# Idle products, SBUF-loaded tap diagonals and two moved loads at the start, two moved sums at the end, of a gated S5/H3 mix

## The chip, the cores and the metric

The kernel runs on one core of a Trainium2 chip. The metric is the time of one execution in device microseconds (us); lower is better. The core has five engines that run their own instruction streams: TensorE (PE; its weight loads are shown apart as PEld), VectorE (DVE), ScalarE (ACT), GpSimd (POOL) and SyncE (SP). DMAs are issued from the instruction streams of SP, ACT and POOL.

## The reference, cut to what matters

```python
x = A_x                                            # [1, 2048, 1024], bfloat16
g = sigmoid((x * gate_w).sum(-1, keepdims=True))
# a: a diagonal complex state space model with 1024 states
dt = exp(log_dt); Lam = Lambda_re + 1j * Lambda_im
Lam_bar = exp(dt * Lam); B_bar = ((Lam_bar - 1) / Lam)[:, None] * (B_re + 1j * B_im)
h[t] = Lam_bar * h[t - 1] + B_bar @ x[t]           # 2048 steps
a = 2 * real(h @ Cmat.T) + x * Dskip
# b: four taps along time, a product, a long convolution over 2048 steps, a product
k_shift[t] = sum(k[t - i] * shift_k[:, i] for i in range(4))
kv = k_shift * v
b = x * (causal_convolution(kv, ssm_k) + kv * ssm_D)
return g * a + (1 - g) * b
```

## The kernel before, in words

Part b works on eight blocks of 128 channels. For a block, `load_k` transposes k into the tile `kk` (channels on partitions, time along the row), and `tap_unit` makes the four taps on TensorE: a diagonal matrix `w` of tap weights times `kk`, shifted by 0 to 3 steps, summed in PSUM (`taps`). For block 0 these are 16 products of 128x128 by 128x512, eight for each half of the time axis; ScalarE copies each half to `ks`. VectorE multiplies `ks` with v (`vT`) in `times_v`. Then the block is folded (`kf`, `vf`, turned by TensorE into `psf` and copied to `eok`, `eov`), taken to its spectrum with tables of cosines and sines (`CF`, `SF`; products `psK`, `psV`, copied to `Kr`, `Ks`, `Vh`), multiplied there on VectorE and taken back (`psz`, `cv`) into a scratch tensor in HBM, `cv_scr`.

Part a cuts the time axis by its remainder r modulo 8, and the states into 16 blocks q of 64, real and imaginary parts on 128 partitions. `B_unit(q)` turns a block of B (`Bst`, loaded by `load_B`) with a small matrix of the columns (`L`, made on VectorE by `matrices`) into `BT`, by way of PSUM `psB` and a copy on ScalarE. `step_unit` multiplies the transposed x (`xT`) with `BT` (`bu`), and the states run through carries, a scan and, last, `Cy`: the states times C into `psy`, one tile of 128 rows of the output after another. `gate(r)` makes the sums for g from `xT` and `gz`.

The start is written out by hand at the end of the function: loads, then `step(ft)` (tables), `vectors()` (a product that turns the rows of log_dt and Lambda into columns, `pcol`), `step(mv)`, `step(sc)` (the state columns `cw`), `step(mv)`, `tap_weights(0)`, the taps of block 0, `gate(0)`, and then B, fold and spectrum of block 0. `more_vectors` (`mv`) turns by 13 small products the rows `skr` (tap weights), gate_w and D (`gsr`) into columns: of `skr` eight for `tcol` (the blocks 1 to 7) and four for `dcol` (block 0), one product for `gz` and `sDc`. `tap_weights(0)` then makes four diagonals on ScalarE from the identity and `dcol`.

Every engine's instructions stand in the order in which the code records them: `put` makes each follow the one before it on its engine. So an instruction that waits holds all that stands behind it on its engine. Nearly every row of the profile therefore has the line of `put`, L99, and the rows are told apart by the names of their tiles. DMAs are issued by `move` (SP), `small` (ACT) and `hop` (POOL). A DMA may also wait for an older one that uses the same counter, of which there are eight for SP and ACT together and eight for POOL.

At the end the last tile of rows is made as two halves of 512 columns, the last two entries of `ends`. For each half `row_scale` (ScalarE) prepares `pair` and `gd` (the scaled convolution and D), and `row_mix` does three things on VectorE: add `gd`, multiply with x, and add the scaled `psy` in a SCALAR_TENSOR_TENSOR; then SP stores the half.

Buffers come from pools by name: `s2` has 33 slots, `psum` four of 128x2x512 in f32.

## Time and profile before

| what | value |
|---|---|
| runs shown | 408.44, 409.61, 413.74 us (median 409.61) |
| the profiled execution | 408.37 us |
| its span, from the first to the last instruction | 406.6 us |
| PE, DVE, ACT, POOL busy | 379.7, 326.7, 251.2, 37.2 us |
| first product on PE, first tap | 5.33 us, 8.81 us |
| last product of PE ends, last store is issued | 401.1 us, 403.51 us |

All times inside a profile count from the span's start. A timeline row has the start, the time from the start to the end of the last of its instructions, the engine (with a q for its instruction queue, which issues DMAs), the line, the operation, the tiles written and read, shapes, how many instructions were merged, and in brackets the engine's idle time before it and what ended that. Matmuls are pipelined, so one lasts longer than the distance to the next.

### The profile page before, as it was taken

To read this page: it belongs to the slowest core of one execution; us is meant where nothing else is said; L and a number is where in the kernel's file an instruction comes from. 1 tells how busy PE (TensorE), PEld (TensorE's weight loads), DVE (VectorE), ACT (ScalarE), POOL (GpSimd) and SP (SyncE) were. 2 spreads that over 40 slices of the span, in tenths; PEclk is the share of its full clock that TensorE was granted. 3 is DMA by queue.
4 is the path that set the end of the run, shared out by engine and by line. 5 is a ranking of instruction groups with operands and counts; after the bars stand their busy time and mean duration, and the time that the engine had idled before them with its cause. 6 is when DMAs were issued, how large, how long until landed. Compare 5 with 4: busy or idle time off the path is not lost.

```text
span 406.6 us, 6769 instructions
## 1 busy us (share of the span) xinstructions
PE 379.7 (93%) x2630; PEld 238.2 (59%) x2630; DVE 326.7 (80%) x421; ACT 251.2 (62%) x321; POOL 37.2 (9%) x77
## 2 busy tenths in 40 slices
PE   2889998999899999999997999978999999999994
PEld 1458976567577768787675775444444444444441
DVE  6853896988969999679694889996897999577554
ACT  5883686856795874695726865385734449265760
POOL 2201000522240221000012000100000000000000
PEclk9999999999999999999999999999999999999999
DMA  8999989999699367905999789995760130888742
GB/s 156 218 209 215 220 179 197 143 223 152 65 222 241 85 122 168 178 21 105 239 205 189 158 147 233 228 151 117 157 188 5 60 84 19 232 264 235 218 122 76
DMA packets 136272, 65.51 MB, mean 161 GB/s; under 512 B 117672, under 2 KB 123824, under 8 KB 136240
## 3 DMA queue, kind: packets, MB, share of 16 engines
q1 hardware_dynamic: 127712, 50.62, 60.5%
q0 software_dynamic: 3888, 6.33, 10.4%
q10 hardware_dynamic: 4640, 8.14, 7.1%
q8 instruction: 20, 0.33, 0.3%
q14 instruction: 12, 0.10, 0.1%
HBM read 19.68 MB, written 11.01 MB: 75 GB/s over the span
## 4 chain that ended last, share of the span: by engine, by line
PE 55%; DVE 8%; ACT 4%; DMA 4%; issue 4%; SPq 1%; ACTq 1%; DVEq 0%; POOLq 0%
PE psy L99 24%; PE bu L99 15%; PE psz L99 4%; PE psV L99 4%; PE psK L99 3%; DVE G L99 3%; PE psT L99 3%; DMA CT<-CT 2%; PE taps L99 2%; ACT h L99 1%; DMA kk<-kk 1%; DVE tmp L99 1%; DVE a L99 1%; SPq L99 1%; DVE T L99 1%
## 5 line engine op out<-in xcount | busy, mean ns | idle before, releaser
L99 PE MATMUL bu<-xT,BT 128*128 128x256 bf16 x1024 | 116.9, 273 | 3.2 <-ACT Kr L99 2.9
L99 PEld LDWEIGHTS <-BT 128*128 128x128 bf16 x1024 | 99.6, 98 | 20.8 <-issue 5.3
L99 PE MATMUL psy<-CT,h 128*128 128x512 bf16 x448 | 98.7, 379 | 2.8 <-DMA CT<-Cim 2.8
L99 PEld LDWEIGHTS <-h 128*128 128x128 bf16 x448 | 43.7, 98 | 56.1 <-DMA CT<-Cim 2.3
L99 ACT ACTIVATE h<-bu 128x1024 bf16<-128x1024 f32 x28 | 28.5, 1022 | 39.1 <-PE bu L99 38.7
L99 ACT ACTIVATE Vh<-psV 128x1024 bf16<-128x1024 f32 x32 | 31.7, 1047 | 4.6 <-PE psV L99 4.6
L99 DVE TENSOR_TENSOR G<-G,tmp 128x3072 bf16<-128x3072 bf16 (+2 forms) x24 | 29.4, 1225 | 0.8
L99 DVE TENSOR_TENSOR T<-T,tmp 128x3072 bf16<-128x3072 bf16 (+2 forms) x24 | 29.4, 1225 | 0.8
L99 ACT ACTIVATE cv<-psz 128x1024 bf16<-128x1024 f32 x16 | 16.4, 1027 | 21.5 <-PE psz L99 10.4
L99 ACT ACTIVATE h<-psT 128x1024 bf16<-128x1024 f32 x28 | 27.9, 1027 | 2.8 <-PE psK L99 1.2
L99 DVE TENSOR_TENSOR tmp<-Kp,Vh 128x3072 bf16<-128x3072 bf16 (+2 forms) x24 | 29.3, 1221 | 0.4
L99 DVE TENSOR_TENSOR G<-Kr,Vh 128x4096 bf16<-128x4096 bf16 x8 | 18.3, 2288 | 12.4 <-ACT Vh L99 12.4
L99 POOL DMA_DIRECT2D kk<-kk x21 | 11.0, 529 | 167.9 <-DMA kk<-in_B_k_dram 110.4
L99 PE MATMUL psT<-h,ident 128*128 128x256 bf16 x112 | 25.6, 273 | 0.0
L99 PEld LDWEIGHTS <-L 128*128 128x128 bf16 x224 | 21.9, 98 | 5.0 <-ACT cv L99 0.7
L99 PE MATMUL psz<-T,CI 128*128 128x512 bf16 x64 | 24.3, 379 | 0.0
L99 PE MATMUL psz<-T,SI 128*128 128x512 bf16 x64 | 24.3, 379 | 0.0
L99 PE MATMUL taps<-kk,w 128*64 128x512 bf16 (+1 forms) x128 | 19.7, 399 | 3.9 <-ACT w L99 2.3
L99 ACT ACTIVATE pairx<-pairx,omg 128x1024 bf16<-128x1024 bf16 (+1 forms) x12 | 11.6, 966 | 18.7 <-DMA pairx<-cv_scr 18.7
L99 PEld LDWEIGHTS <-CF 128*128 128x128 bf16 x128 | 12.0, 98 | 18.0 <-issue 6.9
L99 POOL DMA_DIRECT2D glog<-grow x32 | 18.1, 651 | 36.8 <-ACT grow L99 35.4
L99 ACT ACTIVATE gd<-drow,glog 128x512 bf16<-128x512 bf16 (+1 forms) x25 | 20.7, 827 | 0.0
(161 smaller groups left out, 574.2 us busy)
## 6 DMA issues: line engine op xcount, KB each, us to landing
kn<-in_B_ssm_k_dram SPq DMA_DIRECT2D x8, 512.0 KB, 4.9
cv_scr<-cv ACTq DMA_DIRECT2D x16, 256.0 KB, 3.6
kk<-kk POOLq DMA_DIRECT2D x14, 255.9 KB, 5.6
h_scr<-h ACTq DMA_DIRECT2D x10, 256.0 KB, 3.2
h<-h_scr SPq DMA_DIRECT2D x10, 256.0 KB, 3.2
CT<-Cim SPq DMA_DIRECT2D x16, 128.0 KB, 3.1
out_dram<-ga SPq DMA_DIRECT2D x16, 128.0 KB, 2.8
Bst<-in_A_B_re_dram SPq DMA_DIRECT2D x14, 128.0 KB, 3.4
```

The costliest lines, as they stand in the source:

```text
L99: i = f(*a, **kw)
```

## The change

Five edits. (1) VectorE's first instruction sets a tile `zeros` to 0, and TensorE multiplies it with itself into a PSUM tile that nothing reads: 11 products of 128x128 by 128x512 ahead of `vectors()`, and 5 behind the 9 small products of `more_vectors`, just ahead of the first taps. (2) Block 0's tap weights come from a load of their own, `dcol_b`, 128 partitions by 4, over GpSimd's queue; the four small products into `dcol` go; VectorE, not ScalarE, makes the four diagonals, and does so ahead of the copies to `gz` and `sDc`. (3) The load of the rows `skr` goes from SP's queue, where it stood ahead of `load_k(0)`, to GpSimd's queue, behind the integer tables. (4) `load_B(1)` goes from ScalarE's queue to GpSimd's. (5) In the last tile of rows, the add and the multiply of both halves come ahead of the first half's SCALAR_TENSOR_TENSOR.

```diff
-    move(skr, B_shift_k.rearrange("(j p) k -> j p k", p=128))
+    dcol_b = s2([128, KS], "dcolb")
...
+    zeros = s2([128, 512], "zeros")
+    fill(zeros, 0.0)
     pih, magic = cst([128, 1], "pih"), cst([128, 1], "magic")
...
     trow_i = iota([128, 512], [[1, 2], [M // 2, 2], [2, NR], [M, 512 // M]] if NR > 1 else
                   [[1, 2], [2, 2], [M, 512 // M]], 0, 0, "trow_i")
+
+    hop(dcol_b, B_shift_k[0:128, :])
+    hop(skr, B_shift_k.rearrange("(j p) k -> j p k", p=128))
...
+    def idle_products(n):
+        ps = ps2([128, 2, 512], "pz")
+        for _ in range(n):
+            mm(ps[:, 0], zeros[:, 0:128], zeros, True, True)
+
...
-        for k in range(KS):
-            mm(psp[:, 0, 96 + k:97 + k], skr[:, :, k], ident[0:ND, 0:1], True, True)
         mm(psp[:, 0, 64:64 + 2 * ND], gsr, ident[0:2 * ND, 0:2 * ND], True, True)
         yield
-        copy(dcol, psp[:, 0, 96:96 + KS])
         copy(gz[:, :, 0], psp[:, 0, 64:64 + ND])
...
             lds["w", c] = s2([128, KS, 128], "w0")
+            copy(dcol, dcol_b)
             for p in range(KS):
-                act(lds["w", c][:, p], ident, func=ACT.Copy, scale=dcol[:, p:p + 1])
+                ts(lds["w", c][:, p], ident, dcol[:, p:p + 1], None, ALU.mult)
...
+    def row_ready(t_, h0, h1):
+        pair, gd = ios[t_, h0]
+        tt(pair[:, 0], pair[:, 0], gd, ALU.add)
+        tt(pair[:, 1], pair[:, 1], pair[:, 0], ALU.mult)
+        ios[t_, h0] = pair, None
+
+    def row_mix(t_, h0, h1):
+        if ios[t_, h0][1] is not None:
+            row_ready(t_, h0, h1)
+        pair, _ = ios.pop((t_, h0))
...
     load_B(0, small)
-    load_B(1, small)
+    load_B(1, hop)
...
     step(ft)
+    idle_products(11)
     vectors()
     step(mv)
     step(sc)
+    tap_weights(0)
     step(mv)
-    tap_weights(0)
+    idle_products(5)
     step(sc)
...
             late_row(k)
             k += 1
+        if i + 2 == len(ends):
+            row_ready(*e)
+            row_ready(*ends[i + 1])
         row_mix(*e)
```

On GpSimd, at the start of its stream, there stood before, behind the integer tables (`trow_i` is the last; `gz` is the tile for the gate's columns, `H` the carry tiles):

```order
L213 IOTA trow_i 128x512
L99 MEMSET gz 128x256
L99 MEMSET H_157 128x4x2
L99 MEMSET H_158 128x4x2
L99 MEMSET H_159 128x4x2
L99 MEMSET H_160 128x4x2
L99 DMA glog<-grow 128x1x2 x4
```

and now (`dcolb` and `rows` are the two forms of the tap weights, `Bst` a block of B):

```order
L215 IOTA trow_i 128x512
L99 DMA dcolb<-in_B_shift_k_dram 128x4
L99 DMA rows<-in_B_shift_k_dram 8x512
L99 MEMSET gz 128x256
L99 MEMSET H_161 128x4x2
L99 MEMSET H_162 128x4x2
L99 MEMSET H_163 128x4x2
L99 MEMSET H_164 128x4x2
L99 DMA Bst<-in_A_B_re_dram 64x1024
L99 DMA Bst<-in_A_B_im_dram 64x1024
L99 DMA glog<-grow 128x1x2 x4
```

Two loads of tap weights went ahead of the fills, and two of B ahead of the first `glog`.

On VectorE, between the state columns and the taps, there stood before (`jrow` is the last of the columns' own instructions ahead of the tap weights):

```order
L99 TENSOR_TENSOR II<-ident 128x64
L99 TENSOR_SCALAR jrow<-jrow_i 128x128
L99 COPY dcol<-p 128x4
L99 CAST gz<-p 128x8
L99 COPY sDc<-p 128x8
L99 TENSOR_TENSOR cw<-pcol 128x32
```

and now, with the copy from the loaded `dcolb` and the four diagonals `w` in the copy's place, ahead of `gz`:

```order
L99 TENSOR_TENSOR II<-ident 128x64
L99 TENSOR_SCALAR jrow<-jrow_i 128x128
L99 CAST dcol<-dcolb 128x4
L99 TENSOR_SCALAR w_246<-ident,dcol 128x128 x4
L99 CAST gz<-p 128x8
L99 COPY sDc<-p 128x8
L99 TENSOR_TENSOR cw<-pcol 128x32
```

The diagonals that ScalarE made behind its table load are now five instructions in VectorE's stream, and `gz`, `sDc` and all the columns stand behind them.

On VectorE at the very end, the piece of the difference is this (`pairx` is the first half of the last tile of rows, `pair` the second):

```order
 L99 TENSOR_TENSOR pairx<-pairx,gd 128x512
 L99 TENSOR_TENSOR pairx<-pairx 128x512
+L99 TENSOR_TENSOR pair<-pair,gd 128x512
+L99 TENSOR_TENSOR pair<-pair 128x512
 L99 SCALAR_TENSOR_TENSOR pairx<-psy,glog,pairx 128x512
-L99 TENSOR_TENSOR pair<-pair,gd 128x512
-L99 TENSOR_TENSOR pair<-pair 128x512
 L99 SCALAR_TENSOR_TENSOR pair<-psy,glog,pair 128x512
```

The second half's two sums went ahead of the instruction that waits for the last products. Between the start, up to the first row tiles of B, and this place, the streams of all engines hold the same instructions in the same order.

More of the change, by code (lines that the diff above doesn't have):

```diff
@@ L751, in row_cv, with row_scale @@
                  cv_scr[4 * h0:4 * h1, odd, w * n:(w + 1) * n, tl, kk * NR + u].rearrange("c p d -> p c d"))
-    def row_scale(t_, h0, h1, summed=False):
+    def row_scale(t_, h0, h1):
         pair = ios[t_, h0]
@@ L757, in row_scale @@
         act(gd, drow[:, 512 * h0:512 * h1], func=ACT.Identity, scale=gcols[:, gcol(t_)])
-        if summed:
-            gather(pair[:, 0], gd)
-            gd = None
         ios[t_, h0] = pair, gd
-    def row_mix(t_, h0, h1, summed=False):
-        pair, gd = ios.pop((t_, h0))
+    def row_ready(t_, h0, h1):
[7 more added lines that the diff above has]
+        pair, _ = ios.pop((t_, h0))
         hd = slice(512 * h0, 512 * h1)
-        if gd is not None:
-            tt(pair[:, 0], pair[:, 0], gd, ALU.add)
-        tt(pair[:, 1], pair[:, 1], pair[:, 0], ALU.mult)
         if t_ in gas:
             o = gas[t_][:, hd]
-            if summed:
-                gather(o, pair[:, 1])
-            else:
-                tt(o, o, pair[:, 1], ALU.add)
+            tt(o, o, pair[:, 1], ALU.add)
         else:
```

## The prediction

> **What bounds the kernel now.** I read the page's engine rows first, then the stretches by window, then PE's waits and the timelines of the two places that the change touches. The page:
>
> ```profile
> PE 379.7 (93%) x2630; PEld 238.2 (59%) x2630; DVE 326.7 (80%) x421; ACT 251.2 (62%) x321; POOL 37.2 (9%) x77
> ```
>
> The windows (columns: length, busy time and count of PE, PEld, DVE, ACT, POOL, clock, DMA share, GB/s):
>
> ```profile
> 5.00:8.80 3.80, 0.88 (x14) 0.78 (x14) 3.00 (x22) 2.68 (x10) 0.00 (x0) 1.00 1.21 213
> 14.10:29.20 15.10, 12.64 (x118) 8.29 (x119) 11.16 (x19) 15.06 (x17) 2.29 (x4) 1.00 1.11 209
> 65.00:105.00 40.00, 37.98 (x308) 26.00 (x309) 33.54 (x40) 29.09 (x41) 12.28 (x22) 1.00 1.10 167
> 279.00:401.10 122.10, 122.10 (x576) 55.90 (x572) 94.11 (x116) 67.76 (x80) 0.00 (x0) 1.00 0.51 140
> ```
>
> TensorE is the bound over most of the span: 93% busy, 38.0 of 40 us from 65 to 105, and without a gap from 279 to 401.1. But from 14.1 to 29.2 it is ScalarE, busy 15.06 of 15.10 us; there PE waits for copies. So a gain at the start counts as far as ScalarE's row of copies starts earlier, and a gain at the end counts behind 401.1. The start's timeline:
>
> ```profile
> 0.81 0.06 DVE L99 MEMSET pih<- 128x1 f32 x1 [0.81 <-PEq L1232]
> 2.62 0.30 POOL L99 MEMSET gz<- 128x256 bf16 x1
> 5.33 0.22 PE L99 MATMUL p<-ident,rows 48*128 48x48 bf16 x1 [5.33 <-DVE rows L99]
> 5.85 0.66 PE L99 MATMUL p<-ident,rows 8*64 8x8 bf16 x13 [0.30 <-DVE pcol L99]
> 7.91 0.16 DVE L99 COPY dcol<-p 128x4 f32<-128x4 f32 x1
> 8.37 1.26 ACT L99 ACTIVATE w<-ident,dcol 128x128 bf16<-128x128 bf16 x4
> 8.81 5.28 PE L99 MATMUL taps<-kk,w 128*128 128x512 bf16 x16 [2.29 <-ACT w L99]
> 9.53 0.29 ACT L99 ACTIVATE cw<-cw 128x128 f32<-128x128 f32 x1
> 10.29 0.36 DVE L99 TENSOR_TENSOR cw<-cw 128x64 f32<-128x64 f32 x2 [0.66 <-ACT cw L99]
> 11.77 0.15 PEld L99 LDWEIGHTS <-w 128*128 128x128 bf16 x1 [0.28 <-issue]
> 12.19 1.40 PEld L99 LDWEIGHTS <-w 128*128 128x128 bf16 x7 [0.27 <-issue]
> 12.25 1.23 DVE L99 TENSOR_TENSOR L<-II,cols 128x1024 bf16<-128x1024 bf16 x1
> 14.12 1.02 ACT L99 ACTIVATE ks<-taps 128x1024 bf16<-128x1024 f32 x1 [0.71 <-PE taps L99]
> 14.35 0.62 PE L99 MATMUL psB<-L,Bst 128*128 128x128 bf16 x8
> 15.04 0.40 ACT L99 ACTIVATE grow<-p 128x256 f32<-128x256 f32 x1
> 15.32 1.94 ACT L99 ACTIVATE BT<-psB 128x1024 bf16<-128x1024 f32 x2
> ```
>
> The sixteen taps take 5.28 us, from 8.81 to 14.09. Their weight loads stand 0.42 us apart (11.77 to 12.19) and (1.40 - 0.10) / 6 = 0.217 us apart behind it: PE starts at half its pace, and becomes fast 3.4 us after it has dense work. ScalarE's copy of the second half (14.12) waits for them, and everything on ScalarE behind it follows at once: `grow`, and the first `BT` at 15.32. That is the time by which I measure the start.
>
> **The change part by part.** *Idle products.* The fill of `zeros` takes VectorE's first place (0.81) and lasts between the 0.06 of a 128x1 fill and GpSimd's 0.30 for `gz`, so PE starts near 1.2. Paced as the taps were, it has eight products at 0.42 until about 4.6 and three at 0.217: done at 5.3, when `vectors()` could start anyway (5.33). The price is then 0. If the fast pace doesn't come, 11 x 0.42 = 4.6 us end at 5.8, and `vectors()` and all columns are 0.5 late. The other five cost 5 x 0.217 = 1.08 us on the path to the taps, or 2.1 slow.
>
> *The rows over GpSimd's queue.* The small products wait for them, and behind these on PE stand the five idle products and the taps. Issue and landing on this queue:
>
> ```profile
> 15.75 2.29 POOL L99 DMA_DIRECT2D glog<-grow  x4 [12.69 <-ACT grow L99]
> L99 POOL DMA_DIRECT2D glog<-grow x32: 534/537/1408, 15.8 to 135.2; - x32
> DMA to landing us min/median/max: 2.8/4.2/8.3
> ```
>
> The last two rows are those of `glog`, the 32 smallest transfers of this queue (issue in ns, landing in us). One issue is 2.29 / 4 = 0.57 us; `dcol_b` is issued at 2.62, where the fill of `gz` stood, the rows at 3.19. No row shows such a load from HBM this early; the bounds are 2.8 and 8.3 us, and I take the median 4.2, since the DMA share of 1.21 between 5 and 8.8 is like that of other stretches (1.11, 1.10). The rows land at R = 3.19 + 4.2 = 7.4 (6.0 to 11.5).
>
> The issue itself may be held: the longest in the row takes 1.41, 0.87 more than the median. VectorE works next to it on these:
>
> ```profile
> 3.26 0.62 DVE L99 TENSOR_SCALAR hf<-frf,colm 128x256 f32<-128x256 f32 x2
> 3.91 0.43 DVE L99 TENSOR_SCALAR rq<-hf 128x512 f32<-128x512 f32 x1
> ```
>
> With 0.87 more, R is 8.3. The Trainium skill, "SBUF — State Buffer", section "SBUF: two separate sides", speaks against this move: GpSimd can't write the descriptors of its DMAs while VectorE runs copies or products with scalars in its fast modes. Held through both rows, 0.62 + 0.43 = 1.05, R would be 8.45 by that rule. The trace bears it out little: the median issue is 0.003 above the shortest, whatever VectorE did. I keep 7.4 and give the hold a chance below.
>
> Nine of the thirteen small products take 0.66 x 9 / 13 = 0.46, the idle ones 1.08: the first tap stands at R + 1.54 = 8.94, 0.13 later than now. At the fast pace the taps last 15 x 0.217 + 0.38 (mean of one such product, below) = 3.63 and end at 12.57, not 14.09; the copy starts at 12.60, `BT` could start 1.20 us later (14.12 to 15.32): 13.80.
>
> ```profile
> L99 PE MATMUL psy<-CT,h 128*128 128x512 bf16 x448 | 98.7, 379 | 2.8 <-DMA CT<-Cim 2.8
> ```
>
> *The diagonals on VectorE.* ScalarE loses 1.16 us (8.37 to 9.53), so its sine of the columns, which ended VectorE's wait at 10.29, is ready near 9.1. VectorE gets four products of 128x128 in its row. Bounds by its own distances:
>
> ```profile
> 9.42 0.21 DVE L99 TENSOR_SCALAR sg<-sg 128x1 f32<-128x1 f32 x2
> 14.79 0.34 DVE L99 TENSOR_SCALAR SF<-CF,sg 128x512 bf16<-128x512 bf16 x1
> 15.05 0.34 DVE L99 TENSOR_SCALAR CF<-SF,sg 128x512 bf16<-128x512 bf16 x1
> ```
>
> Between 0.10 for one column (two in 0.21) and 0.26 for 512 (14.79 to 15.05) I take 0.13, near the small end, since the tile is a quarter as wide: 0.52 us. VectorE comes to 10.29's place at 9.63 + 0.52 = 10.15 instead of waiting until 10.29: `L` is 0.14 earlier (0.26 to -0.38 by the bounds), ends at 13.34, the eight `psB` products take 0.62, and with 0.03 for each of two hand-overs (14.09 to 14.12) `BT` starts at 14.02. This is later than 13.80, so it counts: **the start gains 15.32 - 14.02 = 1.30 us** (0.8, with the slow end of the diagonals, to 1.5, with the taps as the bound). The copy of `dcol_b` is wanted on VectorE at 7.91 and it lands at 2.62 + 4.2 = 6.8; `w` is ready by 8.5. `gz`, `sDc` and the columns stand behind these, and `gz` also behind the row products (7.9).
>
> *What is hidden.* The fill of `gz` moves to about 3.8 and is wanted near 8.5. `load_B(1)`, two issues behind the fills of `H`, is out by 5.5 and is wanted by PE at 14.0; even 8.3 us of landing end at 13.8. SP's queue is 0.46 us shorter ahead of `kk`, which nobody waits for: the taps waited for `w`. And there is a side effect, since the counters move on by three: v no longer waits for xT.
>
> ```profile
> 7.85 0.58 SPq L99 DMA_DIRECT2D Bst<-in_A_B_im_dram  x1
> 11.85 2.35 SPq L99 DMA_TRANSPOSE vT<-in_B_v_dram  x1
> 16.54 1.22 DVE L99 TENSOR_TENSOR ks<-ks,vT 128x2048 bf16<-128x2048 bf16 x1 [1.05 <-DMA vT<-in_B_v_dram]
> ```
>
> SP's 3.4 us hold goes, and with it most of VectorE's 1.05. I count it at nothing: ScalarE is full there, and this cover hides it.
>
> *On the way to the end.* PE's later waits could eat the gain. The first that a DMA ends, in the chain of waits:
>
> ```profile
> 99.39 5.22 DMA kk<-kk
> 104.65 1.05 PE taps L99 x8
> ```
>
> A copy of k is issued once its predecessors have landed, and those were issued once PE had done the previous taps; so it starts earlier with PE. I pass the gain on whole (bounds: nothing, or all).
>
> *The last row.*
>
> ```profile
> 401.15 0.75 DVE L99 SCALAR_TENSOR_TENSOR pairx<-psy,glog,pairx 128x512 bf16<-128x512 f32 x1 [2.33 <-PE psy L99]
> 401.82 0.41 DVE L99 TENSOR_TENSOR pair<-pair,gd 128x512 bf16<-128x512 bf16 x1
> ...
> 402.73 0.75 DVE L99 SCALAR_TENSOR_TENSOR pair<-psy,glog,pair 128x512 bf16<-128x512 f32 x1
> 403.51 0.33 SPq L99 DMA_DIRECT2D out_dram<-pair  x1
> ```
>
> The sums from 401.82 to 402.73 go into the 2.33 us in which VectorE waits for PE; the profile names no other thing that it waits for. The last SCALAR_TENSOR_TENSOR then starts 0.67 behind the first (401.15 to 401.82), where the add stood: **0.91 us off the end**, store and all. PE then bounds it, and the store of the second half follows that of the first more closely.
>
> The sum: 1.30 + 0.91 = 2.21. The profiled execution took 408.37 us (span 406.6), just below the lowest run (408.44) and 1.24 below the median (409.61). Against itself it gives 406.2, against the median 407.4; I take 406.8.
>
> **The clock, and a rule.** One window of 0.01 us in which the granted clock (0.70, a mean of 1 and 0.5) changes:
>
> ```profile
> 404.70:404.71 0.01, 0.00 (x0) 0.00 (x0) 0.00 (x0) 0.00 (x0) 0.00 (x0) 0.70 0.44 104
> ```
>
> PE's clock halves at 404.70, 3.6 us behind its last product, and its pace doubled at 12.19, 3.4 us into dense work. The Trainium skill, "TensorE: Matmul & The Clock Gate", section "What's actually happening", says that a monitor looks at PE in windows of 3413 ns which run on their own and don't start with the kernel. The trace agrees: 404.70 - 12.19 = 392.5 us, 115.0 such windows. By that rule whether 4.6 us of idle products hold one whole busy window is a matter of phase.
>
> **The rivals.** *The idle products don't bring the fast pace* (phase, or zeros don't count; for: 3.4 us were needed once, and only 4.1 to 4.6 us of idle work precede a pause until R; against: the pause is shorter than the 3.6 us at the end). Then columns are 0.5 late, the five idle products take 2.1, and the taps start at 7.86 + 2.1 = 9.96. Dense from 7.86, PE is fast at 11.3 in the best case: three slow taps and thirteen fast ones end at 14.3, 0.2 late; one window of 3.4 later, 15.9, 1.8 late. With the end's 0.91 this gives 407.7 to 409.3; 408.5.
>
> *The issue is held*, by the 0.87 above: R = 8.3, `BT` at R + 1.54 + 3.66 + 1.20 = R + 6.40 = 14.7, a gain of 0.6 there, 406.9.
>
> *The rows land late* (the other side). By the same sum the start gains nothing from R = 8.9 on, and the kernel is slower than before from R = 9.8. At the slowest landing, 8.3, R = 11.5 and `BT` is at 17.9: 2.6 lost, 0.91 won, 410.1. For: the load is issued as `kk` and xT fill the DMA engines. Against: the median.
>
> *The gain is eaten on the way*: the copy of k lands at 104.60 all the same, since DMA share is 1.10 there. Only the end's 0.91 is left: 407.5.
>
> **How the numbers follow.** Forecast 0.42 (its own range 405.9 to 407.9: 0.8 to 1.5 at the start, either reference), slow pace 0.23, held issue 0.07, late rows 0.12, eaten 0.14, else 0.02. All lie within 405 and 410; the low end leaves room for v's earlier load, the high end for late rows: 405.0 to 410.1. Two per cent, about what a measurement of this kernel can tell from no change, is 8.2 us: no case reaches it. Faster 0.01, same 0.97, slower 0.02.
>
> **What would show it.** Right: loads of `zeros` 0.42 apart, then 0.217 before 5.3; taps at 0.217 from about 8.9 to 12.6; first `BT` near 14.0; PE's last product at 401.1 - 1.3 = 399.8, and the two SCALAR_TENSOR_TENSOR behind it 0.67 apart. Wrong: a small product that waits for `rows` beyond 8.9, taps 0.42 apart, or a wait of PE for `kk` near 104 that has grown by what the start won.

## The result, and the profile after

The changed kernel took 404.88 us by the median of 20 runs, the kernel before 408.47 us beside it; the ratio of the two is 0.9938, 95% interval 0.9914 to 0.9961, so 1.6 to 3.5 us were gained. The executions of a kernel fall into a faster and a slower state; ratios and intervals use the faster runs of both kernels, medians use all runs. The forecast had a gain of 2.21 us. A second set of runs, on another occasion, gave 0.9914 (0.9877 to 0.9951).

The profiled execution of the changed kernel took 403.2 us, with a span of 401.4. First its engine row of the page: PE was busy 5 us longer than before, in a span that is 5.2 us shorter; the products of zeros alone take 5.8 us (the rows of `pz` below).

```profile
PE 384.7 (96%) x2642; PEld 240.3 (60%) x2642; DVE 327.5 (82%) x426; ACT 250.0 (62%) x317; POOL 39.6 (10%) x81
```

The start on PE, by the timeline of the changed kernel:

```profile
1.19 4.57 PE L99 MATMUL pz<-zeros 128*128 128x512 bf16 x11 [1.19 <-DVE magic L99]
5.70 0.19 PE L99 MATMUL p<-ident,rows 48*128 48x48 bf16 x1
7.11 0.52 PE L99 MATMUL p<-ident,rows 8*64 8x8 bf16 x9 [1.22 <-DVE cw L99]
7.55 1.25 PE L99 MATMUL pz<-zeros 128*128 128x512 bf16 x5
8.76 3.63 PE L99 MATMUL taps<-kk,w 128*128 128x512 bf16 x16
14.03 1.05 PE L99 MATMUL psB<-L,Bst 128*128 128x128 bf16 x16 [1.30 <-DVE kn L99]
```

The taps take 3.63 us, as forecast to the hundredth, and end at 12.39 instead of 14.09. But behind them PE now waits 1.30 us for VectorE. The releaser that is named for the small products at 7.11 had long been done (it is an operation on `cw`); the rows of tap weights landed at 7.06. The same start on VectorE and ScalarE:

```profile
3.92 0.68 DVE L99 TENSOR_SCALAR rq<-hf 128x512 f32<-128x512 f32 x1
8.44 0.74 DVE L99 TENSOR_SCALAR w<-ident,dcol 128x128 bf16<-128x128 bf16 x4
10.69 0.35 DVE L99 TENSOR_TENSOR cw<-cw 128x64 f32<-128x64 f32 x2
12.65 1.23 DVE L99 TENSOR_TENSOR L<-II,cols 128x1024 bf16<-128x1024 bf16 x1
14.67 1.94 ACT L99 ACTIVATE BT<-psB 128x1024 bf16<-128x1024 f32 x2 [0.93 <-PE psB L99]
```

`L` is at 12.65, later than before (12.25), and the first `BT` at 14.67: 0.65 us sooner than before (15.32), where 1.30 was forecast. ScalarE now stands idle for 0.93 us ahead of it.

The end, where VectorE and SP are to be read together:

```profile
397.19 0.75 DVE L99 SCALAR_TENSOR_TENSOR pairx<-psy,glog,pairx 128x512 bf16<-128x512 f32 x1 [1.53 <-PE psy L99]
397.86 0.74 DVE L99 SCALAR_TENSOR_TENSOR pair<-psy,glog,pair 128x512 bf16<-128x512 f32 x1
...
398.63 0.33 SPq L99 DMA_DIRECT2D out_dram<-pair  x1
```

The last two operations stand 0.67 us apart; the last store is issued 1.44 us behind the first of them, against 2.36 before (401.15 to 403.51).

Between start and end, PE's waits of before for `kk` near 104 (1.58 us) and for `Cim` near 274 and 277 (2.8 us together) are gone. This is the group row of the products that had waited 2.8 us (busy time and mean ns, then the idle time before them):

```profile
L99 PE MATMUL psy<-CT,h 128*128 128x512 bf16 x448 | 98.5, 379 | 0.0
```

And this is PE's longest wait that is left, near 219 us, from the list of waits (in total, times, longest):

```profile
PE bu L99 <- ACT Kr L99: 2.8, 1, 2.8
```

So the profiled pair differs by 5.2 us of span, of which the first product on `bu` (27.23 before, 26.58 after) shows 0.65, the middle 3.3 (4.6 us less idle time of PE, from which 1.7 goes by the clock, as worked out below; 0.4 I don't place), and the stretch behind PE's last product 1.2. The 5.2 us of this one pair is more than the 1.6 to 3.5 us that all runs show; the experiments say why.

### The profile page after: what moved, and what is told of

It is laid out like the page before. It is cut to its first block, busy times and chain, and to the rows that moved or that the text cites. A ratio compares the mean times of both kernels' runs of the same rounds, so it can differ in the third digit from the quotient of the medians.

```text
span 401.4 us, 6800 instructions
## 1 busy us (share of the span) xinstructions
PE 384.7 (96%) x2642; PEld 240.3 (60%) x2642; DVE 327.5 (82%) x426; ACT 250.0 (62%) x317; POOL 39.6 (10%) x81
## 4 chain that ended last, share of the span: by engine, by line
PE 85%; ACT 7%; DMA 3%; DVE 3%; ACTq 1%; issue 1%; SPq 1%; DVEq 0%
PE bu L99 29%; PE psy L99 28%; PE psV L99 7%; PE psz L99 6%; PE psK L99 5%; PE psT L99 4%; PE taps L99 3%; DMA Cim<-in_A_C_im_dram 2%; PE pz L99 1%; ACTq L99 1%; ACT h L99 1%; DMA CT<-CT 1%; ACT BT L99 1%; ACT Kr L99 1%; DVE cw L99 1%
## 5 line engine op out<-in xcount | busy, mean ns | idle before, releaser
L99 PE MATMUL bu<-xT,BT 128*128 128x256 bf16 x1024 | 118.6, 275 | 3.1 <-ACT Kr L99 2.8
L99 ACT ACTIVATE cv<-psz 128x1024 bf16<-128x1024 f32 x16 | 16.4, 1027 | 16.8 <-PE psz L99 10.2
L99 PEld LDWEIGHTS <-SF 128*128 128x128 bf16 x128 | 12.1, 98 | 13.6 <-issue 2.2
```

The source lines that it names most:

```text
L99: i = f(*a, **kw)
```

## The experiments

Twelve more runs were made, one of them the changed kernel again. The theory that I tested (A in the expectations) is that a start term and an end term make the gain and add up. Against it stood that only the end pays (B), that the loads on other queues pay in the middle (C), that the zeros don't matter (D), and that the diagonals had held the taps (E). Times are medians; ratios are to the kernel before on the same chip.

| kernel | us | ratio (95%) | first `BT`, us |
|---|---|---|---|
| changed kernel, first set | 404.88 | 0.9938 (0.9914 to 0.9961) | 14.67 |
| changed kernel again | 404.19 | 0.9914 (0.9877 to 0.9951) | 14.98 |
| before + end only | 406.16 | 0.9958 (0.9924 to 0.9993) | 15.87 |
| before + zeros only | 406.66 | 0.9975 (0.9947 to 1.0003) | 14.24 |
| before + zeros + end | 406.26 | 0.9928 (0.9894 to 0.9961) | 14.26 |
| changed, no zeros | 409.06 | 0.9972 (0.9926 to 1.0018) | 15.08 |
| changed, diagonals on ScalarE | 404.78 | 0.9925 (0.9890 to 0.9960) | 16.84 |
| changed, rows on SP's queue | 404.92 | 0.9922 (0.9894 to 0.9950) | 14.99 |
| changed, `sg` late | 404.22 | 0.9915 (0.9877 to 0.9952) | 13.89 |
| `sg` late + denser zeros | 406.50 | 0.9963 (0.9919 to 1.0007) | 13.64 |
| the same + trigonometry late | 404.71 | 0.9889 (0.9840 to 0.9937) | 13.69 |
| the same + `sg` in gaps | 404.00 | 0.9890 (0.9850 to 0.9930) | 15.02 |
| changed + trigonometry late | 406.40 | 0.9944 (0.9905 to 0.9982) | 14.99 |

An interval here is 2 to 4 us wide, so parts of under 1 us are read from the profiles, and the totals only say whether they agree. A profile is one execution: the first `BT` of the table goes with that execution and not with the median beside it.

### The changed kernel again

No edit.

> The changed kernel once more, unaltered, beside the kernels of this call. It separates what its own profiled run showed by chance from what it has each time. Theory A (the gain is start plus end): the two last SCALAR_TENSOR_TENSOR are 0.67 us apart again and the store issues 1.4 us after the first; the first BT copy is at 14.67 if the granted clock rises before the taps (at 4.6 to 8.8), and near 16 if it rises only after them, for the raise stood 5.33 and 5.58 in two kernels with these zeros and 13.86 in a third. Theory C (the middle pays, through the loads on other queues): PE has no wait over 0.5 us at kk near 104 and at Cim near 274, as in its first profile; theory A allows such a wait here, since it takes them for accidents of the queues. Total 404 to 406.5.

Its profile spans 400.0 us, and PE has no wait at `kk` or `Cim` again. The zeros end later this time, and what follows is late by as much:

```profile
6.00 0.22 PE L99 MATMUL p<-ident,rows 48*128 48x48 bf16 x1
7.50 0.51 PE L99 MATMUL p<-ident,rows 8*64 8x8 bf16 x9 [1.28 <-DMA rows<-in_B_shift_k_dram]
```

The trace's record of the granted clock begins with full clock at 5.33 us in the first profile and at 6.73 in this one, with the same instructions up to there. So 11 zeros take 4.57 us or 4.88 as it happens to fall, and the first `BT` moves with it. The end's two operations are 0.67 us apart again (395.78 and 396.45).

### The end alone

```diff
+        if i + 2 == len(ends):
+            row_ready(*e)
+            row_ready(*ends[i + 1])
         row_mix(*e)
```

> The kernel before with only the last edit: the sums and products of the last two rows written before the last PSUM group is read (row_ready). Theory A (the gain is a start term and an end term that add): the two last SCALAR_TENSOR_TENSOR stand about 0.7 us apart and the store issues 1.4 us after the first of them begins, against 2.36 us in the kernel before, so 0.9 us less (407.5 by the median before of 408.5, ratio 0.998); the start is as in the kernel before (first taps at 10.46, first BT copy at 15.32, first bu product at 27.23) and so are the waits for kk near 104 (1.58 us) and for Cim near 274 and 277 (1.02 and 1.78 us). Theory B (only the end pays, the rest is the clock's luck): the whole gain of 2.5 us (ratio 0.994) is here already. Theory C (the middle pays, where loads come sooner): none of the waits at 104 and 274 changes here, and the total moves by 0.9 us at most.

Its timeline at the taps and at the end:

```profile
8.81 5.83 PE L99 MATMUL taps<-kk,w 128*128 128x512 bf16 x16 [2.30 <-ACT w L99]
...
403.83 0.75 DVE L99 SCALAR_TENSOR_TENSOR pairx<-psy,glog,pairx 128x512 bf16<-128x512 f32 x1 [1.53 <-PE psy L99]
404.50 0.74 DVE L99 SCALAR_TENSOR_TENSOR pair<-psy,glog,pair 128x512 bf16<-128x512 f32 x1
```

The end is as forecast. B falls as far as the profile goes: the total, 0.3 to 3.1 us less, doesn't exclude it, but the start gains in other kernels are seen directly. The waits in the middle are not those of the kernel before, as A and C both had it: none for `kk` near 104, 0.8 us for `Cim` instead of 2.8, and one of 2.60 for a copy of `h` near 98. The surprise is the start, which is the code of the kernel before: the taps took 5.83 us here and 5.28 in the profile of before, because the full clock came at 13.30 instead of 12.17. So the 15.32 against which I measured the start was the better of two profiles of the old start.

### The zeros alone, and with the end

```diff
+    idle_products(11)
     vectors()
...
     tap_weights(0)
+    idle_products(5)
```

> The kernel before with the products of zeros alone (11 ahead of the vector products, 5 ahead of the taps, and the memset): no new load, the diagonals on ScalarE, the end as before. Theory A (the zeros raise the clock, and that alone shortens the taps): if the clock rises before the taps, they take 3.63 us instead of 5.28, and the first BT copy comes at 13.7 to 14.4 instead of 15.32; if it rises after them, nothing is gained, or up to 0.5 us is lost to the five slow products (2.1 us) that then stand ahead of the taps. Total 0 to 1.3 us below the kernel before (ratio 0.997 to 1.0). Theory G (the zeros need the new load and VectorE's diagonals beside them, for the taps wait for the diagonals): the taps begin at 8.8 or later all the same and are fast, and the gain is theory A's; the two part only in the taps' begin, 8.4 to 8.8 by G. The waits near 104 and 274 stay as in the kernel before by theory C.

The start of this kernel on PE and ScalarE, which scales the diagonals as before:

```profile
5.33 0.19 PE L99 MATMUL p<-ident,rows 48*128 48x48 bf16 x1
8.78 3.86 PE L99 MATMUL taps<-kk,w 128*128 128x512 bf16 x16 [1.11 <-ACT w L99]
14.24 1.02 ACT L99 ACTIVATE BT<-psB 128x1024 bf16<-128x1024 f32 x1
```

The zeros alone bring the first `BT` to 14.24, earlier than the whole change does (14.67 and 14.98). Most of that lead is the vector product, which is at 5.33 here (full clock came at 4.43) and at 5.70 there: from it to `BT` are 8.91 us here and 8.97 there. The taps begin within 0.02 us of those of the changed kernel (8.76) though nothing was done for the diagonals, as G had it too (its zeros end at 7.67, and PE waits for ScalarE). So the other edits at the start bought nothing that these profiles show. PE's waits of before for `kk` near 104 and for `Cim` near 274 are absent from this profile too, though its queues are the old ones: that they are gone in the changed kernel can't be put down to the new queues. With the end's edit added:

> The kernel before with two parts of the change alone: the products of zeros, and the sums of the last two rows written sooner. No load of its own for the diagonals, which ScalarE scales as before, and no edit to the queues. Theory A (start and end add up, and the rest of the change is worth nothing or costs a little): first BT copy at 14.2 to 14.3 if the clock rises before the taps, as in e5_zeros_only (14.24), against 14.67 and 14.98 in the two profiles of the changed kernel; the last two SCALAR_TENSOR_TENSOR 0.67 us apart; total 2.0 us below the kernel before (1.08 at the start and 0.91 at the end), so as fast as the changed kernel or 0.4 us faster. Theory C (the loads on GpSimd's queue and the diagonals on VectorE carry the gain): the total stays within 1 us of the kernel before, and 1.5 us or more above the changed kernel.

The first `BT` is at 14.26, the end's operations stand 0.66 us apart (403.62 and 404.28), and the ratio is 0.9928: 1.6 to 4.3 us gained, like the changed kernel's 1.6 to 3.5 and 2.0 to 5.0. The single parts give 0.42% and 0.25%, together 0.67%, and the pair 0.72%. A holds in what the runs can resolve, and C, which had the pair within 1 us of before, doesn't.

### Without the zeros

```diff
-    idle_products(11)
     vectors()
...
-    idle_products(5)
```

> The changed kernel without its 16 products of zeros; all else stays, the diagonals on VectorE and the queues too. Theory A (the products of zeros raise the clock before the first taps): the granted clock rises only some 3.4 to 6.8 us after the first taps begin, the 16 taps take 5 to 6.5 us instead of 3.63, and the first BT copy comes at 15.5 to 17 instead of 14.67; the total is 1 to 2 us above the changed kernel. Theory D (the zeros don't matter, since PE waits for VectorE's kn behind the first taps anyway, 1.30 us in the changed kernel): the vector products come 0.4 us sooner (5.33 instead of 5.70), the taps are slower by at most the 1.30 us of that wait, and the first BT copy stays within 0.3 us of 14.67.

Its taps, and a wait in the middle:

```profile
8.67 5.17 PE L99 MATMUL taps<-kk,w 128*128 128x512 bf16 x16 [1.01 <-DVE w L99]
...
107.86 1.49 PE L99 MATMUL taps<-kk,w 128*64 128x512 bf16 x6 [5.36 <-DMA kk<-kk]
```

The taps are slow again, so it was the zeros that made them fast. The ratio falls back to 0.9972, but its interval holds no gain as well as the changed kernel's, so the total doesn't decide. Full clock came at 11.83, 3.2 us into the taps, which is sooner than in the two profiles of the old start (3.4 and 4.5), so D's margin of 0.3 us at `BT` is missed by 0.1 only. The last row speaks against theory C too: this kernel has all the new queues, and its wait for `kk` is the longest of all. In nine profiles with the new queues (the run with the rows on SP's queue left out), PE waited more than 1.5 us somewhere between 90 and 110 us in three; in four with the old queues, in three. That may be a difference or luck, and I leave it open; it isn't a thing that the new queues do each time.

### The diagonals on ScalarE again

```diff
-                ts(lds["w", c][:, p], ident, dcol[:, p:p + 1], None, ALU.mult)
+                act(lds["w", c][:, p], ident, func=ACT.Copy, scale=dcol[:, p:p + 1])
```

> The changed kernel with the four diagonals of the first taps scaled by ScalarE again, from the same load of their own column. Theory A (VectorE's row of work sets the first kn, and with it the second PSUM group and the first BT copy: the four diagonals took 0.74 us of it): VectorE reaches cw some 0.7 us sooner (about 10.0 instead of 10.69), L comes at 11.9 to 12.1 instead of 12.65, and the first BT copy at 13.9 to 14.2 instead of 14.67, unless ScalarE, which is then busier, holds the taps: four ScalarE diagonals took 1.3 us or so in the kernel before. Total 0.3 to 0.7 us below the changed kernel. Theory E (the diagonals were what held the taps, so VectorE is the right place): the first taps begin later than 8.76 by up to 0.6 us and the first BT copy is at 14.7 or later.

Its start on PE and VectorE:

```profile
5.99 0.22 PE L99 MATMUL p<-ident,rows 48*128 48x48 bf16 x1
8.04 2.31 PE L99 MATMUL pz<-zeros 128*128 128x512 bf16 x5
10.15 5.46 PE L99 MATMUL taps<-kk,w 128*128 128x512 bf16 x16
10.95 0.36 DVE L99 TENSOR_TENSOR cw<-cw 128x64 f32<-128x64 f32 x2 [0.65 <-ACT cw L99]
12.92 1.22 DVE L99 TENSOR_TENSOR L<-II,cols 128x1024 bf16<-128x1024 bf16 x1
```

Two things. First, `L` stands 12.92 - 5.99 = 6.93 us behind the vector product. In the kernel before it is 12.25 - 5.33 = 6.92, in the changed kernel 12.65 - 5.70 = 6.95, with the diagonals on VectorE. It makes no difference who scales them: on VectorE they take 0.66 us of its row, on ScalarE they hold the sine for which VectorE then waits 0.65. My theory's 0.7 us for undoing them was wrong, and E with it, since the taps here were late by the clock. Second, this is the case in which the zeros don't bring the full clock: it came at 13.86, the five zeros took 2.31 us, and the taps 5.46.

### The rows on SP's queue again

```diff
+    move(skr, B_shift_k.rearrange("(j p) k -> j p k", p=128))
...
-    hop(skr, B_shift_k.rearrange("(j p) k -> j p k", p=128))
```

> The changed kernel with the load of the rows of B_shift_k on SP's queue again, ahead of kk; the column of the diagonals stays on GpSimd's. Theory A (the queue of the rows matters only through their landing, which holds the products on them and, behind those, the five zeros and the taps): rows land sooner than 7.06, at 5.0 to 6.0, and kk later than 6.23, at 6.7 to 7.0; the taps then wait for the last of kk, the diagonals (first one ready at 8.70) and the zeros, and begin at 8.5 to 8.8 instead of 8.76; the first BT copy stays within 0.2 us of 14.67, since VectorE's row sets it. Total within 0.5 us of the changed kernel. Theory L (the later SP queue, all of whose loads then wait 0.4 us longer, is felt in the middle): waits at kk near 104 or Cim near 274 appear that the changed kernel's two profiles do not have, and the total is 1 us or more above it.

Its start on PE:

```profile
6.00 0.22 PE L99 MATMUL p<-ident,rows 48*128 48x48 bf16 x1
6.52 0.52 PE L99 MATMUL p<-ident,rows 8*64 8x8 bf16 x9 [0.30 <-DVE pcol L99]
9.08 3.63 PE L99 MATMUL taps<-kk,w 128*128 128x512 bf16 x16 [0.86 <-DVE w L99]
```

The small products no longer wait for a DMA, but the taps wait for the diagonals, and `BT` is where the second profile of the changed kernel has it (14.98), with the vector product at 6.00 in both; against 14.67 theory A's margin of 0.2 us is missed by 0.1. The queue of the rows isn't felt at the start. Of the waits that L expected none came, but one of 2.70 us for a copy of `h` on ScalarE near 97.

### `sg` behind the first kn

Six operations on 128x1 tiles (`sg`), 0.85 us of VectorE, moved from ahead of `L` to ahead of the scalings that use them.

```diff
-        sg = [cst([128, 1], f"sg{i}") for i in range(3)]
...
         yield
+        sg = [cst([128, 1], f"sg{i}") for i in range(3)]
...
         ts(SF[:, :, 256:512], CF[:, :, 0:256], sg[2], None, ALU.mult)
```

> The changed kernel with the six small operations on sg and gz (about 0.85 us of VectorE from 9.85 to 10.76) written behind the first L and kn instead of ahead of them. Theory A (VectorE's row sets the first kn): L comes 0.5 to 0.9 us sooner than 12.65, PE's wait of 1.30 us behind the taps shrinks to 0.4 to 0.8, and the first BT copy comes at 13.8 to 14.2 instead of 14.67; the first bu product comes as much sooner. Total 0.4 to 0.9 us below the changed kernel (ratio to the kernel before 0.991 to 0.993). Theory F (something else, as the landing of k, sets kn): L does not move by more than 0.1 us, and the total is that of the changed kernel.

Its start on PE, VectorE and ScalarE:

```profile
5.82 0.19 PE L99 MATMUL p<-ident,rows 48*128 48x48 bf16 x1
11.88 1.22 DVE L99 TENSOR_TENSOR L<-II,cols 128x1024 bf16<-128x1024 bf16 x1
13.25 1.05 PE L99 MATMUL psB<-L,Bst 128*128 128x128 bf16 x16 [0.40 <-DVE kn L99]
13.89 1.94 ACT L99 ACTIVATE BT<-psB 128x1024 bf16<-128x1024 f32 x2
```

`L` is now 6.06 us behind the vector product, and `BT` at 13.89, in spite of a vector product that is 0.12 us later. F falls: VectorE's row is what sets the start of the changed kernel. Two distances hold in all these profiles: the first `BT` starts 2.02 us behind `L` (14.67 - 12.65) or 1.23 us behind the end of the taps (15.32 - 14.09), whichever is later. For the end alone that gives 14.64 + 1.23 = 15.87, for the diagonals on ScalarE 15.61 + 1.23 = 16.84, here 11.88 + 2.02 = 13.90.

### Denser zeros

The kernel above with 9 + 3 zeros around the vector product instead of 11 ahead of it.

```diff
-    idle_products(11)
+    idle_products(9)
     vectors()
+    idle_products(3)
```

> The changed kernel with the sg operations behind the first kn (as in e4_sg_late), nine products of zeros instead of eleven ahead of the vector products, and three more behind them, where PE otherwise idles from 5.9 to 7.1 us until the rows land. Theory A: PE is then dense from 1.2 us to the taps, with no hole over 0.3 us, so that whatever the phase of the clock's windows (3.413 us each), a full one lies between 1.2 and 8.1, and the raise comes at 8.1 at the latest; the vector products come at 5.3 to 5.4 instead of 5.70, and the first BT copy at 13.5 to 13.8 instead of 13.89. Total 0.1 to 1.0 us below e4_sg_late, with fewer runs above 406. Theory H (the phase doesn't matter, the load of PE does): the raise can come later than 8.1, and the total is that of e4_sg_late.

Two waits of its start, on VectorE and on PE:

```profile
13.29 0.16 DVE L99 TENSOR_TENSOR kn<-kn,sDc 128x1 bf16<-128x1 bf16 x1 [0.44 <-DMA kn<-in_B_ssm_k_dram]
...
16.62 0.61 PE L99 MATMUL psf<-ident,kf 128*128 128x128 bf16 x8 [1.76 <-DVE tcol L99]
```

`BT` is 0.25 us earlier, as expected, though the vector product came at 5.58 and not at 5.3 to 5.4: it waited for the copy to `rows`, not for the zeros. But the gain is lost at once: VectorE waits for kn's landing, `sg` stands behind that, `tcol` behind `sg`, and PE waits 1.76 us for the PSUM group that the copy to `tcol` frees. The first product on `bu` is at 26.42, against 25.80 with `sg` late alone. Full clock came at 5.52, as it would have with 11 zeros, so this profile doesn't part A from H. The total isn't the 0.1 to 1.0 us lower that A expected (ratio 0.9963 against 0.9915), though the intervals overlap.

### Trigonometry late, with and without the new start

Near 219 us PE waits in all these kernels while ScalarE makes eight pieces of a table ahead of evicting `Kr`. One number of the order puts them behind it.

```diff
-        "tabs": ((3.2, 4.258, 6.522, 7.95), (3.928, 5.78, 5.091, 5.672), (0.0, 3.825, 5.313, 6.2), (2.634, 4.327, 5.39, 3.91)),
+        "tabs": ((3.2, 4.258, 6.522, 7.95), (3.928, 5.78, 5.091, 5.672), (0.0, 3.825, 5.313, 6.2), (4.05, 4.327, 5.39, 3.91)),
```

> e7_warm with the eight th and trq pieces of the fourth group (3.1 us of ScalarE) behind the two Kr copies near 219 us instead of ahead of them. In the changed kernel PE stands there for 2.84 us until ScalarE has evicted Kr, and the granted clock was then halved for one window of 3.41 us. Theory I (a lost window is bought by the wait just ahead of it): PE's wait near 219 falls under 0.5 us, no window near 220 is at half clock, and the total is 2 to 4.5 us below e7_warm, less what comes late next (h copies, P, the fourth group's tables). Theory J (what PE waits for there is given back at a later wait, on DMA or on VectorE's scan): the wait near 219 goes, but PE's waits behind it grow by as much, and the total is within 1 us of e7_warm.

> The changed kernel with one other edit: the eight th and trq pieces of the fourth group behind the Kr copies near 219 us, as in e8_trig_late; the start stays. Theory I (PE's wait of 2.6 to 2.8 us near 219 is a price of its own, and a lost clock window of 1.67 us comes on top in some runs): the wait goes, no window near 220 is lost, and the total is 1.5 to 3.5 us below the changed kernel (404.2 to 404.9 by the median), so 401 to 403. Theory J (given back at later waits): within 1 us of the changed kernel; in the profile, PE's waits between 225 and 275 grow by 2 us or more (they grew by 2.4 us in e8_trig_late: 0.96, 0.78 and 0.69 near 227, 232 and 260).

With the denser zeros, PE's wait near 219 is 0.38 us, and a wait for `kk` of 3.94 near 106 spoils that profile. Its median is 1.8 us below that of the denser zeros, between what I and J expect, and the intervals overlap. With the changed kernel's start, PE's waits by the timeline:

```profile
221.87 3.65 PE L99 MATMUL bu<-xT,BT 128*128 128x256 bf16 x32 [1.20 <-ACT Kr L99]
231.58 1.61 PE L99 MATMUL psK<-eok,SF 128*128 128x512 bf16 x4 [1.76 <-DMA Cim<-in_A_C_im_dram]
```

1.20 + 1.76 = 2.96 us of waits stand where 2.84 stood. The total is 406.40, 1.5 to 2.2 us above the changed kernel's own medians, 0.2 to 1.2 by the ratios, where theory I had 1.5 to 3.5 below: I falls, and J is right in kind, since PE's time comes back as waits behind it.

### `sg` in VectorE's gaps

The kernel with denser zeros and the trigonometry late; the first three `sg` operations go into VectorE's two idle places around `pcol`.

```diff
         copy(prow[:, 64:128], prow[:, 0:64])
+        sg_steps[0]()
+        sg_steps[1]()
...
+        sg_steps[2]()
```

> e8_trig_late with the first three of the six sg operations in the two idle places of VectorE (0.39 us behind its copy of rows, 0.28 us behind pcol in the changed kernel), the other three ahead of the SF and CF scalings as in e8_trig_late. In e7_warm all six stood between kf and tcol, and PE waited 1.76 us for the PSUM group that tcol's copy frees. Theory A (VectorE's row of work is the bound at the start, and each operation on it counts by its place): kf's second group is waited for some 0.5 us less than in e7_warm and e8_trig_late (1.76 and 1.41), the first BT copy stays at 13.6 to 13.8, and the first bu product comes at 25.2 to 25.6 instead of 25.84. Theory K (the landing of kn, for which VectorE waited 0.44 us in e7_warm, is the bound): the first bu product stays at 25.8 or later. Total: 0 to 0.6 us below e8_trig_late; with no wait on kk near 105 (3.94 us there in that profile), 400 to 404 (ratio 0.985 to 0.991).

It has the lowest median of all, 404.00 us, and with the kernel that it is made from the lowest ratio, 0.989; against the changed kernel (0.9914 to 0.9938) the intervals overlap, so that it beats the kernel before is shown, that it beats the changed kernel is not. K wasn't decided, since this profile's start went wrong in a way that no theory had. PE's timeline:

```profile
1.19 3.47 PE L99 MATMUL pz<-zeros 128*128 128x512 bf16 x9 [1.19 <-DVE magic L99]
7.43 2.32 PE L99 MATMUL pz<-zeros 128*128 128x512 bf16 x5
9.54 4.25 PE L99 MATMUL taps<-kk,w 128*128 128x512 bf16 x16
```

The first nine zeros became fast at 3.98; the five behind them were slow again.

## The clock, by windows of the traces

Much of this is decided by the phase of the clock, and it can be read from busy time by window. A row has the window, its length, then busy time and count of PE, PEld, DVE, ACT, POOL, and the clock granted in it. Ahead of the first entry of the clock's record the column says 1.00, though nine products in 3.40 us (0.42 apart) are at half pace. The record's entries lie whole multiples of 3.413 us apart in every trace, at places that change from run to run. I cut the windows there. With `sg` in the gaps:

```profile
3.98:7.38 3.40, 2.03 (x16) 0.78 (x14) 3.02 (x15) 1.17 (x8) 1.46 (x8) 1.00 1.14 225
7.40:10.80 3.40, 3.40 (x9) 1.21 (x10) 3.23 (x23) 3.32 (x7) 0.00 (x0) 0.50 1.16 197
```

PE was busy 2.03 us in the first window, 0.58 of it with the tiny 48x48 and 8x8 products, and had half its clock in the next: the taps came into it. With the diagonals on ScalarE:

```profile
3.63:7.03 3.40, 2.58 (x7) 0.69 (x5) 2.26 (x7) 0.74 (x4) 1.81 (x8) 1.00 1.25 212
7.04:10.44 3.40, 2.86 (x15) 1.30 (x16) 2.99 (x23) 3.37 (x12) 0.00 (x0) 1.00 1.09 223
10.45:13.85 3.40, 3.40 (x9) 1.19 (x8) 2.87 (x15) 2.24 (x6) 0.00 (x0) 1.00 1.10 257
```

Here the zeros fell on both sides of a boundary, and neither window was full enough; the third, with taps, was. The same happens in the middle. The changed kernel, twice, at its wait for `Kr` (2.84 us, and 2.64):

```profile
216.96:220.36 3.40, 1.30 (x12) 1.17 (x12) 2.19 (x3) 3.40 (x7) 0.00 (x0) 1.00 1.21 153
220.37:223.77 3.40, 3.40 (x18) 2.42 (x16) 3.33 (x4) 1.95 (x6) 0.00 (x0) 0.50 0.65 132
```

```profile
214.95:218.34 3.39, 1.73 (x12) 1.02 (x11) 0.00 (x0) 2.79 (x9) 0.68 (x1) 1.00 1.29 222
218.36:221.76 3.40, 2.44 (x23) 2.18 (x23) 3.30 (x4) 3.40 (x5) 0.00 (x0) 1.00 1.04 244
```

With 1.30 us busy the next window ran at half clock, with 1.73 it did not. From the first product on `bu` to the last on `psy` the one execution took 370.19 us and the other 368.48, at the same idle time of PE (6.48 and 6.44): a lost window costs 1.7 us. In the profile of the kernel before the same wait of 2.88 us fell so that 1.70 us were busy in its window, and nothing was lost. That is chance, not the kernel; it is one reason why single profiles of the same kernel differ by a few us, and why the pair's 5.2 us isn't the change's worth.

The Trainium skill, "TensorE: Matmul & The Clock Gate", section "HAM oscillation — how this bites in real kernels", gives as the abstract rule that PE should have no idle gap above some 3.4 us. Here the measurement is stricter and decides: gaps of 2.02 us (near 67, diagonals on ScalarE) and 2.84 us (changed kernel) each cost a window where they fell badly. Busy time alone doesn't draw the line: with the rows on SP's queue a window with 1.45 us busy (from 221.59) was followed by full clock, and in the changed kernel with the trigonometry late one with 1.54 (from 228.47) by half of it.

## Why the prediction was right, and which terms were not

**The idle products** did what was said, in most phases: in eight profiles with 11 of them ahead of the vector product, the full clock came before the taps in seven, between 3.9 and 6.8 us, and in one not. I had given the failure 0.23. Their price of 0 was wrong: I let the fast pace come at 4.6, and it came at 5.33 and 6.73, so the vector product was 0.37 and 0.67 us late. That delay goes through to `L`. In the first profile only the last 0.1 of it is the zeros' alone: the copy to `rows` came 0.26 us later too, for a reason given below, and with nine zeros the vector product still stood at 5.58.

**The rows** landed at 7.06 (7.4 in the sum), the first tap stood at 8.76 (8.94), and the taps took 3.63 us. All this was right and is not what counts, because of the next term.

**The diagonals on VectorE** are the step that failed: "`L` is 0.14 earlier". It was 0.40 later, by 0.37 from the columns, 0.14 from the four diagonals (0.66 instead of 0.52) and 0.03 in the rest of VectorE's row. The way from `L` to `BT` was 0.11 longer as well, 2.02 instead of 1.91: `psB` starts 0.15 behind the end of `L` (13.00 against 12.85 with the denser zeros, where `L` is named as the releaser), and the sum had 0.03. Together these are the 0.65 us between 14.02 and 14.67: the start gained 0.65 us where I had 1.30, and 0.34 by the second profile. The experiments show the step itself to be worth nothing: 6.93 us from the vector product to `L` with ScalarE's diagonals, 6.95 with VectorE's. The gain of 0.8 at the slow end of the diagonals was nearer than the value taken.

**What stood against it** is that 15.32 was the better case of the old start; the end alone, with the same start, had 15.87. By the means of 15.32 and 15.87 and of 14.67 and 14.98 the start is worth 0.8 us, with 0.34 to 1.20 from pair to pair: an estimate from four profiles.

**The held issue** didn't come, since the rows landed in time; the two issues on GpSimd's queue took 0.71 and 0.65 us against the median of 0.54, where 0.87 more was feared. It was VectorE that paid, and what held it was not an issue. Its product on `rq` took 0.68 us, as quoted, against 0.43 in the kernel before and with the zeros alone, and the copy to `rows` came 0.26 us later. Beside `rq` stood GpSimd's fill of `gz`, which the change had put behind the two issues:

```profile
3.97 0.34 POOL L99 MEMSET gz<- 128x256 bf16 x1
```

With the rows on SP's queue that fill comes sooner, and then it is `hf` that is long (0.80, against 0.62 before), while `rq` beside an issue takes its old 0.43:

```profile
3.27 0.80 DVE L99 TENSOR_SCALAR hf<-frf,colm 128x256 f32<-128x256 f32 x2
3.32 0.34 POOL L99 MEMSET gz<- 128x256 bf16 x1
3.72 0.55 POOL L99 DMA_DIRECT2D Bst<-in_A_B_re_dram  x1
4.10 0.43 DVE L99 TENSOR_SCALAR rq<-hf 128x512 f32<-128x512 f32 x1
```

So moving the loads ahead of the fills cost the start up to 0.26 us. The Trainium skill, "SBUF — State Buffer", section "SBUF: two separate sides", has the pair of engines in an exclusive lock that whichever starts first keeps; the trace agrees with the lock, as the four fills of `H` behind `gz` took 0.45 us together beside `rq` and 0.20 in the kernel before, but it doesn't show who had it first, since `rq`'s row starts 0.05 us ahead of `gz`'s.

**The end** was right to the hundredth, 0.67 us apart, and 0.92 off the last store's issue; behind the end of PE's last product the span got 1.2 us shorter (5.5 to 4.3), and 0.9 to 1.3 us in all kernels with this edit.

**The gain passed on whole** as far as the totals can tell, and more came in the middle of the profiled pair, by waits for DMAs that were absent. The prediction's price of nothing for the queues can't be proved from that; kernels with the same queues had such waits, up to 5.36 us, and kernels with the old queues were without them. The number of 2.21 is partly luck: the start term was twice what the first profile shows, and an interval of 2 us can't tell 1.30 from 0.65 there. The forecast also stood between two references (408.37 and 409.61) while the rivals were counted from the first alone, so they were some 0.6 us too low beside it. The absolute time lies 0.12 us below the range's low end; the median before had itself come out 1.14 us lower in these runs (408.47) than in the three shown (409.61).

## What to carry to other kernels

Warming TensorE with products of zeros pays where PE would idle anyway, but the phase decides whether it works; making them dense for two windows of 3.4 us, up to the real work, should help, which no run here shows. If they end behind the time at which the next product's operands are ready, the delay goes on to all that follows (up to 0.67 us here). Before an operation is moved to another engine, add up that engine's row to the point where both rows meet: 0.66 us on the one was 0.65 on the other. And measure the start of a kernel from several profiles, since one has one phase.

## What the runs showed of the hardware

- All-zero operands count for the clock: it rose within 2.8 to 5.5 us of the first product of zeros in seven of eight profiles.
- The rise came behind a window with at least 2.68 us of wide products (2.90 less the 0.22 of a 48x48 product, in the second profile of the changed kernel) and not behind 2.58 (denser zeros with the trigonometry late, from 0.37). That the tiny products hardly count is how these numbers fit together: 2.75 us of wide products alone raised the clock (zeros and end, from 0.54), while 2.86 with the nine tiny ones among them didn't (diagonals on ScalarE, from 7.04). It wasn't tried by itself.
- Among the windows up to PE's last product, those with 1.36 us busy or less lost the clock each time, and one with 1.61 (the kernel before, from 275.01) and fuller ones kept it, but for the 2.03 with tiny products; between 1.45 and 1.54 both happened.
- The zeros can hurt: with `sg` in the gaps a rise at 3.98, followed by holes, gave half the clock for 3.4 us just at the taps.
- The third copy of `kk`, issued on GpSimd's queue near 95 to 101 us, landed in 2.9 to 3.2 us in the changed kernel, with the diagonals on ScalarE and with `sg` late, where it went ahead of SP's next transposes, and in 10.2 us without the zeros, where they were issued 0.3 us sooner (97.33 against 97.62). The streams of these kernels are the same there; that the order is the cause wasn't tried.
